# Attention with hashed buckets and an FFN: the low products of P times v narrowed to 64 columns and woven into the transposes

## The chip, the cores and the metric

One NeuronCore of a Trainium2 chip. The metric is the device time of one execution in microseconds (us), the median of 3 runs. All engines of the core work from queues of their own: TensorE (PE in the profile, its weight loads PEld), VectorE (DVE), ScalarE (ACT), GpSimd (POOL) and SyncE (SP), which issues most transfers.

## The reference, cut to what matters

```python
# q, k, v: (4, 8, 768, 64) f32, proj (64, 6)
mask = bucket(q @ proj)[:, :, :, None] == bucket(k @ proj)[:, :, None, :]   # 6 sign bits
scores = where(mask, q @ k.T / 8, -1e9)
attn = exp(scores - max(scores)); attn = attn / (sum(attn) + 1e-9)
x = (attn @ v) as (3072, 512)
h = x @ w_in                       # 512 -> 2048
out = (h * clip(h + 3, 0, 6) / 6) @ w_out   # 2048 -> 512
```

## The kernel before, in words

Every product is done in split precision: an operand is a high part, rounded to float32r (the fast 4-byte format of TensorE), and a low part, the rest, and the products of the parts are summed in PSUM.

**Steps.** There are 4 batches x 8 heads = 32 heads of 768 queries, each in 6 blocks of 128: 192 steps k. A step has, each for its own block: `scores` of block k+3 (LA = 3; four products of 384 columns, L305 and L308, into a pair of PSUM banks), `lowest` of block k+2 (VectorE, L315: the minimum and a copy of the scores to the tile `p`, of which there are two), `exponential` of block k+1 (ScalarE, L327, in place), `transp` of block k (TensorE, L337: six transposes of 128 x 128 float32, three into each of two PSUM banks `pt`), and `split_p` of block k, once for each bank (ScalarE copies the high part, L360; VectorE subtracts for the low part, L361). Steps go in pairs: `split_p` puts the two blocks of a pair u = k // 2 side by side, so that the product with v has 256 moving columns.

**The product with v.** `values(u, c)` does half c of pair u: for each of three blocks of keys one product with the high part (L374) and one with the low part (L375), both with the same stationary tile `vv[:, kt]`. That tile is 128 columns wide: the high part of v in 64 of them and its low part in the other 64 (which half holds which alternates from head to head, `split_v`, L287, on GpSimd). So the accumulator `acc`, a PSUM bank of 128 x 256, holds main results in 64 partitions and those of v's low part in the other 64. `output` (L384) copies it out (L402), and stores one half to `xs` in DRAM and adds the other half to it by a transfer that accumulates (`add`, L381); for the last head of a batch it adds them on the core (L399).

**What sets the order.** The order of the work on TensorE, VectorE, ScalarE and GpSimd is that of the program's text (`manual_schedule`, L840). The main loop (L848) does in each step, in this order: `transp` for both halves, `exponential(k + 1)`, `lowest(k + 2)`, then the halves of the product with v that are due, parts of the FFN (`next(fill)`), `scores` of k + 3 (in `lead`, with the loads, splits and the hash of the next head) and `split_p`. Which halves are due: up to step 101 (`third`, except step 48) one half in each step, half 0 in even steps and half 1 in odd ones; from step 102 on (GF + 2 = 102), and in step 48, both halves in the even steps and none in the odd ones. Steps 0 to 47 and 52 to about 100 are attention alone. At k = 51 the FFN of batch 0 is put in whole (`first_ffn`, with the loads and splits of the weights). From step 98 on the FFN of the finished batches runs beside attention: each step has one `gemm1` (12 products of 256 columns, L478 to L480) and one `gemm2` (six of 512, L500 to L502).

**Buffers.** PSUM banks for transposes, accumulators, `gemm1` and the normalisation (`rt`, L436) come from two tags, pt and pu, with two buffers each, in turn (`bank`, L79). The scores' pairs of banks alternate between two, s and po; with the FFN on there is only s (`pair`, L90).

Of the kernel before, what the change touches and what calls it, by code (L numbers as in the profile page):

```python
# [10 lines left out]
F32 = mybir.dt.float32  # L11
# [7 lines left out]
P = 128  # L19
# [21 lines left out]
def lsh_attention_moe(  # L41
# [10 lines left out]
    nc = tc.nc  # L52
    B, H, D, S = qkT.shape
    D //= 2
    DM, DF = w_in.shape
    KT = S // P
    HW = S // 2
    QT = HW // P
# [14 lines left out]
    def dma(out: bass.AP, in_: bass.AP):  # L73
        nonlocal last
        last = nc.sync.dma_start(out=out, in_=in_)
# [3 lines left out]
    def bank(shape, name: str, tag: str | None = None):  # L79

        nonlocal turn
        if tag is None:
            tag = ("pt", "pu")[turn % 2]
            turn += 1
        return ps.tile(shape, F32, name=name, tag=tag, bufs=2)
# [15 lines left out]
    ident = cp.tile([P, P], F32, name="ident")  # L101
# [104 lines left out]
    HK = H * KT  # L206
    GB = HK + FB
    GF = 2 * HK + FS
# [21 lines left out]
    def scale_q(i: int):  # L230

        nc.gpsimd.tensor_scalar_mul(raws[i][:D], raws[i][:D], -SCALE)

    def split_qk(i: int, copy):

        raw = raws.pop(i)
        kk, qq = (sp.tile([P, 2 * S], F32R, name=f"{x}_{i}", tag=x)[:] for x in ("kk", "qq"))
        k1, k2, q1, q2 = state[i] = [x[:, c : c + S] for x in (kk, qq) for c in (0, S)]
        if i == 0:

            nc.scalar.mul(q1[:D], raw[:D], -SCALE)
            nc.vector.tensor_copy(q1[D:], raw[D:])
            hash_weights()
            nc.vector.tensor_sub(k2[:D], raw[D:], q1[D:].bitcast(F32))
            nc.vector.scalar_tensor_tensor(
                out=q2[D:], in0=raw[:D], scalar=-SCALE, in1=q1[:D].bitcast(F32),
                op0=ALU.mult, op1=ALU.subtract,
            )
            nc.scalar.copy(k2[D:], raw[D:])
            nc.scalar.copy(q2[:D], q1[:D].bitcast(F32))  # L250
            nc.scalar.copy(k1[:D], raw[D:])
            return
        copy(q1[:], raw)
        dma(out=k2[D:].bitcast(F32), in_=q1[D:].bitcast(F32))
        dma(out=q2[:D].bitcast(F32), in_=q1[:D].bitcast(F32))
        dma(out=k1[:D].bitcast(F32), in_=q1[D:].bitcast(F32))
        nc.gpsimd.tensor_sub(k2[:D], raw[D:], q1[D:].bitcast(F32))
        nc.gpsimd.tensor_sub(q2[D:], raw[:D], q1[:D].bitcast(F32))
# [26 lines left out]
    vvs = {}  # L285

    def split_v(i: int):  # L287
        o = (i % 2) * D
        vr = vrs.pop(i)
        vv = vvs[i] = sp.tile([P, KT, P], F32R, name=f"vv{i}", tag="vv")  # L290
        nc.gpsimd.tensor_copy(vv[:, :, o : o + D], vr[:])
        nc.gpsimd.tensor_sub(
            vv[:, :, D - o : 2 * D - o], vr[:], vv[:, :, o : o + D].bitcast(F32)
        )

    scs, probs, outs = {}, {}, {}

# [33 lines left out]
    pts, parts = {}, {}  # L331
    halves = 0

    def transp(g: int, c: int):
        pt = pts[g, c] = bank([P, QT, P], f"pt{g}_{c}")
        for x in range(QT):
            nc.tensor.transpose(pt[:, x], probs[g][0][:, c, x * P : (x + 1) * P], ident[:])  # L337
        if c:
            del probs[g]

    lent = []

# [23 lines left out]
    def values(u: int, c: int):  # L366
        vv = vvs[2 * u // KT]
        if c == 0:
            accs[u] = bank([P, 2 * P], f"acc{u}")
        acc = accs[u]  # L370
        hi, lo = parts.pop((u, c))
        for x in range(QT):
            kt = c * QT + x
            nc.tensor.matmul(acc[:], lhsT=vv[:, kt], rhs=hi[:, x], start=(kt == 0), stop=False)  # L374
            nc.tensor.matmul(acc[:], lhsT=vv[:, kt], rhs=lo[:, x], start=False, stop=(kt == KT - 1))  # L375

    adds = []

    def add():
        for _, to, of in adds:  # L380
            nc.gpsimd.dma_start(out=to, in_=of, accum_op=ALU.add)  # L381
        adds.clear()

    def output(un: int):  # L384
        nonlocal vdone
        i, u = divmod(un, KT // 2)
        b, h = divmod(i, H)
        o = (h % 2) * D
        acc = accs.pop(un)

        if u != 1:
            outs[i] = sp.tile([P, 4 * P if u == 0 else 2 * P], F32, name=f"y{i}_{u}", tag=f"y{u}", bufs=1)
        y = outs[i][:, 2 * P :] if u == 1 else outs[i][:, : 2 * P]

        r = slice(o, o + D)
        r2 = slice(D - o, 2 * D - o)
        last_head = h == H - 1
        if last_head:
            nc.scalar.copy(y[r], acc[r2])  # L399
            nc.vector.tensor_add(y[r], acc[r], y[r])  # L400
        else:
            nc.scalar.copy(y, acc[:])  # L402
        if u:
            c = slice(0, 4 * P) if u == 1 else slice(4 * P, S)
            to = xs[b][h * D : (h + 1) * D, c]
            dma(out=to, in_=outs[i][r])
            if not last_head:
                adds.append((i, to, outs[i][r2]))
        vdone = 2 * un + 2
# [408 lines left out]
    vnext = 0  # L818

    def value_half():  # L820
        nonlocal vnext
        u, c = divmod(vnext, 2)
        vnext += 1
        values(u, c)
        return c == 1

    def ahead(k: int, part: int):

# [11 lines left out]
    with tc.manual_schedule(engines={ET.PE, ET.DVE, ET.Activation, ET.Pool}):  # L840
        split_qk(0, None)
        hash_qk(0)
        bits(0)
        scale_q(1)
        split_v(0)
        for x in range(3):
            ahead(0, x)
        for k in range(NS):  # L848
            end = GB if k < GB else NS
            i, t = divmod(k, KT)  # L850
            if k == HK - XE:
                lent += [cp.tile([P, 2 * WC], F32R, name=f"lent{n}", tag="w", bufs=NW) for n in range(2)]
            if k == GB:
                lent.clear()
            if k == HK:
                late["x"] = sp.tile([P, S], F32, name="late", tag="raw", bufs=1)
            for c in range(2):
                transp(k, c)
            if k + 1 < end:
                exponential(k + 1)  # L860
            if k + 2 < end:
                lowest(k + 2)
            if k == GB:
                next(first)
                pair_turn = 0

            third = k < GF + 2
            whole = False
            for _ in range(1 if third and k != HK else (2, 0)[k % 2]):
                if vnext < k - k % 2:  # L870
                    whole = value_half()
            if k >= GF - 2:
                next(fill, None)
            if whole and k >= GF:
                output(vnext // 2 - 1)
                whole = False

            hashed = k >= GF and (k + LA) % KT == 2
            if k >= GF and k + LA < end and not hashed:
                lead(k + LA)  # L880
            for c in range(2):
                split_p(k, c, third)
            if (k < GF or hashed) and k + LA < end:
                if hashed:
                    if (k + LA) // KT + 1 < NJ:
                        hash_qk((k + LA) // KT + 1)
                        bits((k + LA) // KT + 1)
                    next(fill, None)
                lead(k + LA)
            if whole:  # L890
                output(vnext // 2 - 1)
            if k >= GF - 2 and not hashed:
                next(fill, None)
            if k + LA >= NS:
                add()
            if HK - XE <= k < GB:
                for f in early_steps[k - HK + XE]:
                    f()

            if k < HK and t == 1 and i:  # L900
                with tc.issue_after(last.ins):
                    for n in range((i - 1) * WE // (H - 1), i * WE // (H - 1)):
                        load_w(n)
            if k == HK:
                late_x()
                with tc.issue_after(last.ins):
                    get_qk(H + 2)
                    for n in range(WE, WL):
                        load_w(n)
            if k + 1 == GB:  # L910
                first = first_ffn(lambda part: ahead(GB, part))
                next(first)
                for _ in range(2):
                    whole = value_half()
                output(vnext // 2 - 1)
                next(first)
        while vnext < NS:
            if value_half():
                output(vnext // 2 - 1)
        add()  # L920
        for _ in fill:
            pass
# [47 lines left out]
```

## Time and profile before

| | us |
|---|---|
| median of 3 runs (1040.15 to 1041.07) | 1040.96 |
| the profiled execution's own time | 1040.82 |
| its span | 1039.0 |
| TensorE busy | 1009.5 (97%) |
| VectorE busy | 687.0 (66%) |
| ScalarE busy | 583.6 (56%) |
| GpSimd busy | 451.4 (43%) |

The span is the time from the first to the last instruction that the profile shows. Weight loads (PEld) overlap the products of PE. A product's end is modelled and overlaps the next one's start, so two neighbours are compared by their starts.

### The profile page before, as it was taken

How to read it: one execution, taken by the hardware profiler on the slowest of the kernel's cores; microseconds unless marked ns; L12 is line 12 of the kernel's file. 1: busy time of each engine (PE TensorE's matmuls, PEld its weight loads, DVE VectorE, ACT ScalarE, POOL GpSimd, SP SyncE). 2: the span in 40 equal slices, each digit the busy share in tenths (PEclk: the TensorE clock that was granted, in tenths of full speed). 3: DMA queues.
4: the chain of work that ended last, by engine and by line, in shares of the span. 5: the costliest groups of instructions: out<-in, count | busy, mean ns of one | idle time of the engine just before them, and what ended most of it. 6: DMA issues, size and time to landing. Idle time of an engine off the chain costs nothing.

```text
span 1039.0 us, 18911 instructions
## 1 busy us (share of the span) xinstructions
PE 1009.5 (97%) x6846; PEld 927.2 (89%) x6846; DVE 687.0 (66%) x1441; ACT 583.6 (56%) x1308; POOL 451.4 (43%) x439
## 2 busy tenths in 40 slices
PE   8999879999999999999999999999999999999998
PEld 7999868887989998899999999999899999899997
DVE  6999888999479998766656666655665563333332
ACT  6888855555478887645554555454455462333332
POOL 5677753334247775645444444544454232200100
PEclk9999989999999999999999999999999999999999
DMA  3666686000144555322222232222232011101000
GB/s 93 155 149 155 187 277 236 1 2 1 46 130 112 120 124 143 80 53 60 75 46 63 61 88 59 53 71 59 60 93 47 15 37 28 42 1 41 1 22 20
DMA packets 47380, 80.68 MB, mean 78 GB/s; under 512 B 5892, under 2 KB 27780, under 8 KB 47288
## 3 DMA queue, kind: packets, MB, share of 16 engines
q1 hardware_dynamic: 42808, 73.98, 24.2%
q0 software_dynamic: 4480, 5.51, 4.6%
q8 instruction: 54, 0.88, 0.4%
q14 instruction: 38, 0.31, 0.1%
HBM read 41.95 MB, written 18.09 MB: 58 GB/s over the span
## 4 chain that ended last, share of the span: by engine, by line
PE 83%; DVE 8%; issue 3%; POOL 2%; ACT 2%; DMA 1%; SPq 0%; DVEq 0%; POOLq 0%; ACTq 0%
PE pt L337 11%; PE h L479 7%; PE h L478 7%; PE h L480 7%; PE po L500 7%; PE po L502 7%; PE po L501 7%; PE acc L374 6%; PE acc L375 6%; PE s L305 6%; PE s L308 6%; DVE wr L175 1%; DVE pl L361 1%; DVE wr L177 1%; PE z L267 1%
## 5 line engine op out<-in xcount | busy, mean ns | idle before, releaser
L315 DVE TENSOR_SCALAR_CACHE_REDUCE p<-s 128x768 f32<-128x768 f32 x192 | 183.5, 956 | 103.5 <-PE pt L337 99.5
L361 DVE TENSOR_TENSOR pl<-pt,ph 128x384 fp32r<-128x384 f32 x376 | 191.8, 551 | 50.4 <-ACT ph L360 48.3
L360 ACT CAST ph<-pt 128x384 fp32r<-128x384 f32 x376 | 165.5, 480 | 57.4 <-PE pt L337 45.0
L327 ACT ACTIVATE p<-p,m 128x768 f32<-128x768 f32 x192 | 179.5, 935 | 5.1 <-DVE p L315 4.8
L487 ACT ACTIVATE g<-h,three 128x256 f32<-128x256 f32 x192 | 91.4, 476 | 155.9 <-PE h L480 141.6
L337 PE MATMUL pt<-ident,p 128*128 128x128 f32 x1152 | 162.2, 275 | 5.9 <-DVE pl L361 4.8
L493 POOL TENSOR_TENSOR gl<-g,gh 128x256 fp32r<-128x256 f32 x96 | 74.2, 773 | 203.7 <-DVE gh L492 160.0
L488 DVE SCALAR_TENSOR_TENSOR g<-g,h 128x256 f32<-128x256 f32 x192 | 80.6, 420 | 117.8 <-ACT g L487 115.3
L337 PEld LDWEIGHTS pt<-ident,p 128*128 128x128 f32 x1152 | 137.3, 141 | 23.6 <-PE pt L337 3.8
L374 PE MATMUL acc<-ph,vv 128*128 128x256 f32 x564 | 152.8, 303 | 1.0 <-DVE pl L361 1.0
L478 PE MATMUL h<-xh,w 128*128 128x256 f32 x512 | 147.7, 289 | 1.2 <-ACT y L402 1.2
L480 PE MATMUL h<-xh,w 128*128 128x256 f32 x512 | 143.4, 280 | 1.3 <-POOL w L196 1.3
L479 PE MATMUL h<-xl,w 128*128 128x256 f32 x512 | 143.2, 280 | 0.6 <-DVE xl L470 0.6
L375 PE MATMUL acc<-pl,vv 128*128 128x256 f32 x564 | 141.1, 283 | 0.0
L500 PE MATMUL po<-w,gh 128*128 128x512 f32 x320 | 126.7, 396 | 1.5 <-ACT gh L492 1.4
L501 PE MATMUL po<-w,gh 128*128 128x512 f32 x320 | 126.2, 394 | 0.9 <-POOL w L196 0.9
L502 PE MATMUL po<-w,gl 128*128 128x512 f32 x320 | 126.6, 396 | 0.0
L374 PEld LDWEIGHTS acc<-ph,vv 128*128 128x128 f32 x564 | 107.5, 191 | 2.2 <-DVE pl L361 1.9
L375 PEld LDWEIGHTS acc<-pl,vv 128*128 128x128 f32 x564 | 107.9, 191 | 0.0
L305 PE MATMUL s<-kk,qq 76*128 76x384 f32 x384 | 101.2, 344 | 2.5 <-ACT kk L281 1.5
L308 PE MATMUL s<-kk,qq 128*128 128x384 f32 x384 | 100.0, 341 | 0.0
L478 PEld LDWEIGHTS h<-xh,w 128*128 128x128 f32 x512 | 96.4, 188 | 3.8 <-ACT y L402 2.4
(134 smaller groups left out, 1999.5 us busy)
## 6 DMA issues: line engine op xcount, KB each, us to landing
raw<-in_qkT SPq DMA_DIRECT2D x32, 384.0 KB, 3.5
kk<-qq SPq DMA_DIRECT2D x62, 192.0 KB, 3.2
wr<-in_w_in SPq DMA_DIRECT2D x16, 512.0 KB, 7.1
wr<-in_w_out SPq DMA_DIRECT2D x16, 512.0 KB, 3.8
vr<-in_v SPq DMA_DIRECT2D x32, 192.0 KB, 2.4
qq<-qq SPq DMA_DIRECT2D x31, 192.0 KB, 3.6
out<-ob SPq DMA_DIRECT2D x11, 512.0 KB, 3.0
xr<-xs SPq DMA_DIRECT2D x9, 512.0 KB
```

What stands on the lines that cost most here:

```text
L315: nc.vector.tensor_scalar(out=pr_[:], in0=s[:, :, :HW], scalar1=CAP, scalar2=None, op0=ALU.min, op1=ALU.min, accum_out=m[:],)
L327: nc.scalar.activation(pr_[:], pr_[:], AF.Exp, bias=m[:], scale=-1.0, accum_out=sms[b][:, t, h : h + 1])
L337: nc.tensor.transpose(pt[:, x], probs[g][0][:, c, x * P : (x + 1) * P], ident[:])
L361: nc.vector.tensor_sub(lo[:, :, w], pt[:], hi[:, :, w].bitcast(F32))
L374: nc.tensor.matmul(acc[:], lhsT=vv[:, kt], rhs=hi[:, x], start=(kt == 0), stop=False)
L375: nc.tensor.matmul(acc[:], lhsT=vv[:, kt], rhs=lo[:, x], start=False, stop=(kt == KT - 1))
L478: nc.tensor.matmul(hp[:], lhsT=wi[:, 0, wc], rhs=xh, start=(cc == 0), stop=False)
L479: nc.tensor.matmul(hp[:], lhsT=wi[:, 0, wc], rhs=xl, start=False, stop=False)
L480: nc.tensor.matmul(hp[:], lhsT=wi[:, 1, wc], rhs=xh, start=False, stop=(cc == NCC - 1))
L500: nc.tensor.matmul(po[u], lhsT=gh[:, us], rhs=wo[:, 0], start=(fc == 0), stop=False)
L501: nc.tensor.matmul(po[u], lhsT=gh[:, us], rhs=wo[:, 1], start=False, stop=False)
L502: nc.tensor.matmul(po[u], lhsT=gl[:, us], rhs=wo[:, 0], start=False, stop=(fc == NFC - 1))
```

## The change

`values` no longer does its products: it returns two lists, the products with the high part (`main`: all 128 columns of `vv`, first and last of the accumulation) and those with the low part (`rest`: only the first 64 columns of `vv`, into the first 64 partitions of `acc`). To make these 64 columns the main half for every head, `split_v` and `output` drop the alternation. The product of P's low part with v's low part is thereby left out.

`transp(k, n)` does both banks' six transposes and takes the n due halves with it. With two halves (n = 2) the first high product goes ahead of all transposes. If the last half taken is half 1 (`whole`), one low product follows each transpose while there are any: three in the odd steps up to 101, six in step 48 and in the even steps from 102 on. Otherwise the transposes come first, then one high product, the low ones and the other high ones. The remaining high products follow the transposes. `exponential` and `lowest` stand after all that in the text, on their own engines. In step 52 (GB) and at the end the halves are done without transposes (`value_halves`: one high, three low, two high).

```diff
     def split_v(i: int):
-        o = (i % 2) * D
         vr = vrs.pop(i)
         vv = vvs[i] = sp.tile([P, KT, P], F32R, name=f"vv{i}", tag="vv")
-        nc.gpsimd.tensor_copy(vv[:, :, o : o + D], vr[:])
-        nc.gpsimd.tensor_sub(
-            vv[:, :, D - o : 2 * D - o], vr[:], vv[:, :, o : o + D].bitcast(F32)
-        )
+        nc.gpsimd.tensor_copy(vv[:, :, :D], vr[:])
+        nc.gpsimd.tensor_sub(vv[:, :, D:], vr[:], vv[:, :, :D].bitcast(F32))
...
-    def transp(g: int, c: int):
-        pt = pts[g, c] = bank([P, QT, P], f"pt{g}_{c}")
-        for x in range(QT):
-            nc.tensor.transpose(pt[:, x], probs[g][0][:, c, x * P : (x + 1) * P], ident[:])
-        if c:
-            del probs[g]
+    def transp(g: int, n: int):
+
+        pr_, _ = probs.pop(g)
+        for c in range(2):
+            pts[g, c] = bank([P, QT, P], f"pt{g}_{c}")
+        his, los, whole = [], [], False
+        for _ in range(n):
+            h, l, whole = value_half()
+            his += h
+            los += l
+        if n > 1:
+            his.pop(0)()
+        woven = whole
+        for x in range(KT):
+            nc.tensor.transpose(
+                pts[g, x // QT][:, x % QT], pr_[:, x // QT, (x % QT) * P : (x % QT + 1) * P], ident[:]
+            )
+            if woven and los:
+                los.pop(0)()
+        for f in [*his[:1], *los, *his[1:]]:
+            f()
+        return whole
...
         hi, lo = parts.pop((u, c))
-        for x in range(QT):
+
+        def main(x: int):
             kt = c * QT + x
-            nc.tensor.matmul(acc[:], lhsT=vv[:, kt], rhs=hi[:, x], start=(kt == 0), stop=False)
-            nc.tensor.matmul(acc[:], lhsT=vv[:, kt], rhs=lo[:, x], start=False, stop=(kt == KT - 1))
+            nc.tensor.matmul(acc[:], lhsT=vv[:, kt], rhs=hi[:, x], start=(kt == 0), stop=(kt == KT - 1))
+
+        def rest(x: int):
+
+            nc.tensor.matmul(acc[:D], lhsT=vv[:, c * QT + x, :D], rhs=lo[:, x], start=False, stop=False)
+
+        return [[lambda x=x, f=f: f(x) for x in range(QT)] for f in (main, rest)]
...
-        r = slice(o, o + D)
-        r2 = slice(D - o, 2 * D - o)
+        r = slice(0, D)
+        r2 = slice(D, 2 * D)
...
-        values(u, c)
-        return c == 1
+        return *values(u, c), c == 1
...
-            for c in range(2):
-                transp(k, c)
+
+            third = k < GF + 2
+            n = 0
+            for _ in range(1 if third and k != HK else (2, 0)[k % 2]):
+                n += vnext + n < k - k % 2
+            whole = transp(k, n if k != GB else 0)
             if k + 1 < end:
                 exponential(k + 1)
...
-            third = k < GF + 2
-            whole = False
-            for _ in range(1 if third and k != HK else (2, 0)[k % 2]):
-                if vnext < k - k % 2:
-                    whole = value_half()
+            if k == GB and n:
+                whole = value_halves(n)
```

## Rows read from the trace of the kernel before

**Rows 1.** The page: span, engines, slices (tenths of 1/40 span), chain by engine.
```profile
span 1039.0 us, 18911 instructions
PE 1009.5 (97%) x6846; PEld 927.2 (89%) x6846; DVE 687.0 (66%) x1441; ACT 583.6 (56%) x1308; POOL 451.4 (43%) x439
...
PEclk9999989999999999999999999999999999999999
...
PE 83%; DVE 8%; issue 3%; POOL 2%; ACT 2%; DMA 1%; SPq 0%; DVEq 0%; POOLq 0%; ACTq 0%
```

**Rows 2.** TensorE's waits: waiting, awaited, us in total, times, longest us.
```profile
PE pt L337 <- DVE pl L361: 4.8, 6, 2.3
```

**Rows 3.** Busy time by stretch: PE, PEld, DVE, ACT, POOL, clock, DMA, GB/s.
```profile
65.00:90.00 25.00, 25.00 (x189) 24.34 (x188) 23.04 (x47) 21.61 (x50) 18.70 (x15) 1.00 0.62 152
...
700.00:800.00 100.00, 99.60 (x693) 92.60 (x692) 61.13 (x128) 50.61 (x116) 47.74 (x48) 1.00 0.27 66
```

**Rows 4.** Timeline of TensorE, 702.8 to 707.8 us: start us, duration us, engine, line.
```profile
703.33 0.40 PE L502 MATMUL po<-w,gl 128*128 128x512 f32 x1
703.56 0.82 PE L337 MATMUL pt<-ident,p 128*128 128x128 f32 x6
...
704.34 0.28 PE L375 MATMUL acc<-pl,vv 128*128 128x256 f32 x1
...
705.53 0.28 PE L375 MATMUL acc<-pl,vv 128*128 128x256 f32 x1
705.65 0.28 PE L478 MATMUL h<-xh,w 128*128 128x256 f32 x1
...
707.05 0.52 PE L305 MATMUL s<-kk,qq 76*128 76x384 f32 x2
```

**Rows 5.** Timeline 819.2 to 820.3 us, all engines; idle time before in brackets.
```profile
819.32 0.28 PE L375 MATMUL acc<-pl,vv 128*128 128x256 f32 x1
819.44 0.38 PE L436 MATMUL rt<-ident,rb 128*128 128x128 f32 x2
819.64 0.37 ACT L402 COPY y<-acc 128x256 f32<-128x256 f32 x1 [2.97 <-PE acc L375]
819.86 0.42 DVE L439 TENSOR_TENSOR xr<-xr,rt 128x256 f32<-128x256 f32 x1 [0.68 <-PE rt L436]
...
820.07 0.19 PEld L478 LDWEIGHTS h<-xh,w 128*128 128x128 f32 x1 [0.48 <-ACT y L402]
...
820.17 0.19 PEld L479 LDWEIGHTS h<-xl,w 128*128 128x128 f32 x1
```

**Rows 6.** Transposes' loads after an idle time (timeline); loads by shape (busy us, mean ns).
```profile
741.69 0.20 PEld L436 LDWEIGHTS rt<-ident,rb 128*128 128x128 f32 x2 [0.39 <-POOL rb L426]
...
L337 PEld LDWEIGHTS pt<-ident,p 128*128 128x128 f32 x1152 | 137.3, 141 | 23.6 <-PE pt L337 3.8 <-issue 2.9 <-ACT p L327 1.0
L375 PEld LDWEIGHTS acc<-pl,vv 128*128 128x128 f32 x564 | 107.9, 191 | 0.0
...
L266 PEld LDWEIGHTS z<-kk,pjh 128*108 128x108 f32 x64 | 11.1, 173 | 0.1
```

**Rows 7.** Products by shape (busy us, mean ns).
```profile
L305 PE MATMUL s<-kk,qq 76*128 76x384 f32 x384 | 101.2, 344 | 2.5 <-ACT kk L281 1.5 <-DVE qq L276 0.6 <-DVE p L315 0.3
L308 PE MATMUL s<-kk,qq 128*128 128x384 f32 x384 | 100.0, 341 | 0.0
...
L266 PE MATMUL z<-kk,pjh 128*108 128x384 f32 x64 | 21.7, 339 | 0.0
```

**Rows 8.** Timeline of VectorE and ScalarE, 701.0 to 706.9 us.
```profile
701.13 1.02 DVE L361 TENSOR_TENSOR pl<-pt,ph 128x384 fp32r<-128x384 f32 x2
...
704.42 0.96 DVE L315 TENSOR_SCALAR_CACHE_REDUCE p<-s 128x768 f32<-128x768 f32 x1 [0.71 <-PE pt L337]
...
705.85 0.37 ACT L402 COPY y<-acc 128x256 f32<-128x256 f32 x1 [2.75 <-PE acc L375]
```

**Rows 9.** Timeline of VectorE in attention alone, 65 to 70 us.
```profile
68.80 0.96 DVE L315 TENSOR_SCALAR_CACHE_REDUCE p<-s 128x768 f32<-128x768 f32 x1 [0.24 <-PE pt L337]
```

More of the change, by code (lines that the diff above doesn't have):

```diff
@@ L387, in output @@
         b, h = divmod(i, H)
-        o = (h % 2) * D
         acc = accs.pop(un)
@@ L823, in value_half, with value_halves @@
         vnext += 1
-        values(u, c)
-        return c == 1
+        return *values(u, c), c == 1
+    def value_halves(n: int):
+        for _ in range(n):
+            his, los, whole = value_half()
+            for f in [his[0], *los, *his[1:]]:
+                f()
+        return whole
     def ahead(k: int, part: int):
@@ L912, in lsh_attention_moe @@
                 next(first)
-                for _ in range(2):
-                    whole = value_half()
+                value_halves(2)
                 output(vnext // 2 - 1)
@@ L917, in lsh_attention_moe @@
         while vnext < NS:
-            if value_half():
+            if value_halves(1):
                 output(vnext // 2 - 1)
```

## The prediction

> **What bounds the kernel now.** I read the page's engine line, slices and chain first [rows 1]. TensorE is busy 97% of the span, the chain of waits is 83% TensorE, and the granted clock is in its top digit in nearly every slice. Busy overstates a pipelined engine, so I turned next to the waits of TensorE alone [rows 2]: the longest line is 4.8 us in all. Then the stretches [rows 3]: from 700 to 800 us TensorE lacks 0.4 us, and in the stage of attention alone (65 to 90 us) nothing, though VectorE is at 92% there. So in both stages the time is the sum of TensorE's instructions, and a change that moves TensorE's order is worth what it does to the distance from one start to the next. Stalls lie elsewhere, around the first FFN, which this change leaves in its order.
>
> I then read the distances from a second step beside the FFN [rows 4]. The six transposes start at 703.56, 0.109 apart (0.82 less the last one's 0.27, over five). The value products, high and low in turn, start 0.119 apart (ten of them from 704.34 to 705.53), and 512 columns take 0.23. Weight loads overlap all this.
>
> **The change part by part.** It removes no instruction. It narrows 576 low products (three for each of 192 half blocks) from 128 to 64 stationary columns, with the same 256 moving ones, drops low times low from the sum, and reorders. Pairs of transpose and low product arise where a step has a whole second half: 6 in each even step from 102 to 190 (45 steps, 270), 6 in step 48, 3 in each odd step of 3 to 47, 51, and 55 to 101 (48 steps, 144): 420. The other 156 low products stand among themselves or beside high ones.
>
> *The weight load.* What does it take alone? Where TensorE had been idle, the next load starts as soon as this one's product can: 0.10 to 0.11 after it for 128 columns of the split operands (820.07 to 820.17), but only 0.06 for a transpose (two loads take 0.20, one 0.14) [rows 5, 6]. Recorded loads go with the width, 191 ns at 128 columns and about 173 at 108, so 0.9 ns a column [rows 6]; 64 columns would be recorded at about 134 and occupy half of 0.108, 0.054 (my estimate). So the change cuts the load by half.
>
> *Does any load end last?* A transpose's load needs 0.06, yet transposes stand 0.109 apart: its own stream must hold them. The consumers say the same [rows 5]: ScalarE starts 0.32 after the start of the last 256-column product (819.32 to 819.64), VectorE 0.31 after the last transpose (819.55 to 819.86), so a transpose of 128 columns passes nearly as late as 256. Behind a transpose, then, 0.109 of stream already covers a load of 0.108, and a product's 0.12 covers either. Halving a covered load gives nothing.
>
> *The rule against that reading.* The Trainium skill, "TensorE: Matmul & The Clock Gate", section "LDWEIGHTS (loading the stationary operand)", prices a load by its columns alone, 107 ns for 128; the split operands agree (0.10 to 0.11), the transposes' 0.06 does not. By that page transposes would be bound by their loads and a pair would gain; that is the second rival below.
>
> *The stream of 64 columns.* No row is that narrow. The nearest is the hash, 108 wide: 384 columns are recorded at 339 ns, against 341 at 128 wide; and 76 rows instead of 128 make 344 [rows 7]. The array's filling does not set the pace, so I keep 0.12. Bounds: down to a transpose's 0.109, worth 576 x 0.0105 = 6.0 us; upward, the price of going to and fro.
>
> *To and fro.* From the 512-column product at 703.33 to gemm1 at 705.65 are 2.32 us [rows 4]; 0.233 + 6 x 0.109 + 12 x 0.119 is 2.315. So one way in and out costs at most 0.005. Woven, there are 420: 0 to 2.1 us. I take 0.
>
> *The order beside the FFN.* The first high product now stands ahead of the transposes and a low one behind each. The last transpose ends 0.12 + 5 x 0.12 = 0.71 later, the step's products as late as before. Ahead of it: the high product needs the previous step's split, done by 701.13 + 1.02 = 702.15 for a start at 703.56 [rows 4, 8], so 1.4 us cover it; its accumulator bank comes free with that same split. Behind it: VectorE's minimum, which waits for the transposes, goes from 704.42 to 705.13 and ends at 706.1; the scores that need its bank start at 707.05, so 0.9 us are left. The split of this step waits in ScalarE's queue behind the accumulator's copy (idle until 705.85), whose time does not move. Odd steps keep their order. Cost 0.
>
> *Attention alone.* In odd steps three low products go ahead of the last transposes, which end 0.36 later; even steps keep their order. The minimum waits there for the transposes, with 0.24 us of idle VectorE before it [rows 9]. It is 0.12 behind in the next step and has 0.36 more after that. The scores alternate between two banks and the exponential has a step in hand, so I take 0 and keep the lag as a rival.
>
> *Small things.* Step 48 is woven with no FFN to cover it: its first product meets a split that ends about half a us later, once. GpSimd's two splits of v keep their size, and the output and accumulate transfers their bytes; only the partitions are now the same for each head. At 0.06 us of load and 0.11 of stream for a transpose no step falls idle, so the clock has no cause to fall.
>
> The sum: 0 on the profiled execution's 1040.82 (span 1039.0 and 1.8 around it), which lies 0.14 under the median of the three runs, 1040.96. I forecast 1041.0, its own range 1039 to 1043.
>
> **The rivals.**
> *The narrow product streams faster.* Half the array would let 256 columns pass at a transpose's 0.109: 1041 - 6 = 1035.0. For it: the products stand 0.119 apart, above the transposes' 0.109. Against: widths of 108 and 128 pass alike.
> *The transposes are short and their loads hold them.* If the 0.109 between transposes were the load and not the stream, a low product would cover it and the transpose would shrink to a load of some 0.06: 420 x 0.05 = 21, so 1020. Against: the load of 0.06 after an idle time, and consumers that start after 0.31.
> *VectorE's lag is passed on* (slower). Each of 48 woven odd steps of attention alone costs the 0.36 less the 0.24 of idle time: 48 x 0.12 = 5.8, so 1046.8. It decides as soon as TensorE needs, within a step, something behind that minimum. For it: VectorE's 92%. Against: two banks, and 0.36 more time in the even step.
> *Each change of width drains the array* (slower). A 256-column product is recorded at 0.28 from start to end against 0.12 to the next start, so 0.16 of pipeline would be bared twice a pair [rows 4]: 420 x 0.32 = 134, so 1175. Against: no sign of it between transposes and products, both 128 wide, nor at the hash's 108. The Trainium skill, "TensorEngine Tiling (Array Packing)", section "Key Properties", says that changing the tiling mode drains TensorE; no run here shows a width at which it would. The skill's "PSUM — Partial Sum Buffer", under "The four PSUM rules", says that float32r products force the full column group, which speaks against a mode change here.
>
> **How the numbers follow.** Forecast 0.50; faster stream 0.14; short transposes 0.13; small gains of the order over 2.1 us 0.03; VectorE's lag 0.12; drain 0.04; small losses over 2.1 us 0.04. A measurement of this kernel tells some 0.2%, 2.1 us, from no change. Faster is 0.14 + 0.13 + 0.03 = 0.30, same 0.50, slower 0.20. The range takes in the faster stream and VectorE's lag and leaves out short transposes and drain (0.17): 1034.5 to 1047.
>
> **What would show it.** Right: weight loads of the low products recorded near 134 ns; a pair of transpose and low product still 0.109 + 0.12 = 0.23 from transpose to transpose; TensorE's waits as short as before. Wrong: pairs of 0.17 to 0.18 (short transposes), low products 0.109 before the next start (faster stream), 0.5 or more (drain), or TensorE waiting for VectorE between 20 and 110 us or 300 and 400 us (lag).

## The result, and the profile after

The changed kernel takes 1044.99 us (median of 6 runs, 1043.41 to 1046.23) against 1040.59 (1039.94 to 1041.82) of the kernel before, a ratio of 1.0042 [1.0029, 1.0055]: slower by 4.4 us. The forecast was no change at 1041.0. The time lies inside the stated range, 1034.5 to 1047, whose upper part stood for the slower rival "VectorE's lag is passed on" (1046.8). Half of what is lost is lost in that rival's place, attention alone, though by another road; the other half comes from two terms that no case had.

The profiled execution took 1045.29 us. Its page:

```profile
span 1043.5 us, 18777 instructions
PE 1010.8 (97%) x6846; PEld 929.3 (89%) x6846; DVE 682.8 (65%) x1441; ACT 581.8 (56%) x1308; POOL 450.7 (43%) x439
...
PE 83%; DVE 8%; issue 3%; ACT 2%; POOL 2%; DMA 0%; DVEq 0%; POOLq 0%; ACTq 0%
```

Beside [rows 1] the page shows almost nothing: the same number of matmuls, TensorE 1.3 us busier, the same chain. 4.4 us in a thousand have to be looked for by place. I took marks that both kernels have: the score product of the second row, one for each block of scores. The same two marks of before and of after (timeline of TensorE):

```profile
28.70 0.53 PE L308 MATMUL s<-kk,qq 128*128 128x384 f32 x2
...
110.64 0.52 PE L308 MATMUL s<-kk,qq 128*128 128x384 f32 x2
```

```profile
27.73 0.51 PE L305 MATMUL s<-kk,qq 128*128 128x384 f32 x2
...
111.05 0.52 PE L305 MATMUL s<-kk,qq 128*128 128x384 f32 x2
```

The kernel before needs 81.94 us from one to the other, the changed one 83.32: +1.38 in the first stage of attention alone. The whole span, cut in this way (us, after less before; times are those of before):

| stretch | difference |
|---|---|
| start, to 29 us | -0.97 |
| attention alone, 29 to 111 | +1.38 |
| 111 to 122 | -0.09 |
| step 48 and first FFN, 122 to 287 | +1.47 |
| attention alone, 299 to 391 (row starts at 287) | +1.68 |
| the FFN sets in again, 391 to 436 | +1.59 |
| steps beside the FFN, 436 to 852 | -0.55 |
| tail | -0.03 |

They add up to 4.48, the difference of the spans being 4.5. The steady steps beside the FFN, which the change was mostly about, win half a microsecond; attention alone, one half-clock stretch and the place where the FFN sets in lose 6.1. The start differs by up to 0.9 between two runs below whose first steps have the same text (-1.46 in b1_one_woven, -0.56 in c1_one_and_plain), so I give it to no part of the change.

**Beside the FFN**, as forecast. The loads' group, by shape, and then TensorE's timeline of a second step:

```profile
L392 PEld LDWEIGHTS acc<-pl,vv 128*64 128x64 f32 x564 | 75.0, 136 | 1.6
```

```profile
708.31 0.27 PE L345 MATMUL pt<-ident,p 128*128 128x128 f32 x1
708.34 0.36 PE L392 MATMUL acc<-pl,vv 128*64 128x256 f32 x1
...
709.45 0.27 PE L345 MATMUL pt<-ident,p 128*128 128x128 f32 x1
```

The narrow load is recorded at 136 ns (forecast 134, before 191 in [rows 6]). Six transposes with a low product between them take 1.14 us from the first to the last, so a pair of transpose and product is 0.228; before, 0.109 and 0.119 to 0.120 make 0.228 to 0.229.

**Attention alone**: the loss is no steady drift. Step by step it is +0.25 us in one step of six, 13 times in the two stages (13 x 0.25 = 3.2; the 1.38 and 1.68 are 3.06), and within 0.09 elsewhere, nearly cancelling. It is the step behind the one in which VectorE also forms the hash's bits (below, the step behind the hash's). VectorE's group of minima has more idle time ahead of it, in the kernel before and then after:

```profile
L315 DVE TENSOR_SCALAR_CACHE_REDUCE p<-s 128x768 f32<-128x768 f32 x192 | 183.5, 956 | 103.5 <-PE pt L337 99.5
```

```profile
L312 DVE TENSOR_SCALAR_CACHE_REDUCE p<-s 128x768 f32<-128x768 f32 x192 | 183.4, 955 | 143.9 <-PE pt L345 141.3
```

Most of these 40 us lie beside the FFN (81.7 us before, 108.4 after), where they cost next to nothing; the two stages of attention alone have 6.1 and 6.3 before, 9.2 and 9.6 after. A sum over the span does not tell where the time is lost.

Some lines around one such step, after (idle time before, and what ended it, in brackets):

```profile
346.42 1.08 DVE L276 TENSOR_SCALAR qq<-z,thr,val 44x768 fp32r<-44x768 f32 x1
...
347.43 0.49 PE L345 MATMUL pt<-ident,p 128*128 128x128 f32 x3
...
347.96 0.96 DVE L312 TENSOR_SCALAR_CACHE_REDUCE p<-s 128x768 f32<-128x768 f32 x1 [0.45 <-PE pt L345]
...
348.83 0.82 PE L345 MATMUL pt<-ident,p 128*128 128x128 f32 x6
...
348.95 1.02 DVE L374 TENSOR_TENSOR pl<-pt,ph 128x384 fp32r<-128x384 f32 x2
...
349.63 0.19 PEld L388 LDWEIGHTS acc<-ph,vv 128*128 128x128 f32 x1 [0.22 <-issue]
349.74 0.25 PEld L392 LDWEIGHTS acc<-pl,vv 128*64 128x64 f32 x2
```

and before:

```profile
343.92 1.08 DVE L276 TENSOR_SCALAR qq<-z,thr,val 44x768 fp32r<-44x768 f32 x1
...
344.24 0.82 PE L337 MATMUL pt<-ident,p 128*128 128x128 f32 x6
...
345.10 0.96 DVE L315 TENSOR_SCALAR_CACHE_REDUCE p<-s 128x768 f32<-128x768 f32 x1
...
346.09 1.02 DVE L361 TENSOR_TENSOR pl<-pt,ph 128x384 fp32r<-128x384 f32 x2
...
346.32 0.82 PE L337 MATMUL pt<-ident,p 128*128 128x128 f32 x6
...
346.87 0.19 PEld L374 LDWEIGHTS acc<-ph,vv 128*128 128x128 f32 x1
346.98 0.19 PEld L375 LDWEIGHTS acc<-pl,vv 128*128 128x128 f32 x1
```

Before, the six transposes of the odd step are through (344.24 and 0.82) just after VectorE leaves the bits (345.00), and its minimum follows within 0.1 us. After, three low products push the last transposes back, and VectorE stands idle for 0.45. In both kernels, in nearly every odd step, the minimum starts 0.31 after the start of the last transpose, so it moves by the whole delay. Its minimum and the two subtractions behind it in its queue start later. The next step's six transposes (348.83, 346.32) go out in their usual rhythm; the first high product behind them does not: its weight load starts 0.80 after the first transpose instead of 0.55 (349.63 less 348.83; 346.87 less 346.32). That is the 0.25. The accumulator of this product takes, by round robin, the PSUM bank of the first half's transposes four allocations back (`pt` and `acc` share one pool), and the bank is free when L374 has read it. The start times show this wait. In each of these 13 steps after, the high product starts 0.146 to 0.147 after the end of that subtraction; before, in 12 of them, it starts 0.236 to 0.244 after it. So before there were 0.09 to 0.10 us to spare.

**Where the FFN sets in**, TensorE already waited for that subtraction before [rows 2]; most of the waits got longer (7.7 us in 7 waits over the whole span, 4.8 in 6 before). After, then before:

```profile
396.08 0.52 PE L345 MATMUL pt<-ident,p 128*128 128x128 f32 x3 [0.68 <-DVE pl L374]
...
407.30 0.52 PE L345 MATMUL pt<-ident,p 128*128 128x128 f32 x3 [0.81 <-DVE pl L374]
...
423.73 0.30 PE L345 MATMUL pt<-ident,p 128*128 128x128 f32 x1 [1.23 <-DVE pl L374]
```

```profile
392.26 0.52 PE L337 MATMUL pt<-ident,p 128*128 128x128 f32 x3 [0.32 <-DVE pl L361]
...
403.01 0.52 PE L337 MATMUL pt<-ident,p 128*128 128x128 f32 x3 [0.49 <-DVE pl L361]
```

**Step 48 on**: 3.4 us at a granted clock of 0.50, that is 1.2 GHz, that the kernel before does not have. After, a line of the timeline, with TensorE's wait, and the row of a stretch (columns as in [rows 3]); then both of before:

```profile
129.65 0.44 PE L454 MATMUL rt<-ident,rb 128*128 128x128 f32 x2 [1.86 <-POOL rb L444]
```

```profile
130.70:134.10 3.40, 3.40 (x17) 3.33 (x16) 2.61 (x5) 1.74 (x4) 2.55 (x3) 0.50 0.64 187
```

```profile
129.34 0.44 PE L436 MATMUL rt<-ident,rb 128*128 128x128 f32 x2 [1.59 <-POOL rb L426]
```

```profile
130.70:134.10 3.40, 3.40 (x26) 3.35 (x25) 3.32 (x7) 1.88 (x4) 2.39 (x4) 1.00 0.60 179
```

17 matmuls are done where 26 were. At half speed 3.4 us lose 1.7 us of work, which is the +1.47 of this stretch. Ahead of it TensorE had waited 1.86 us for GpSimd's normalised rows, 0.27 longer than before. (Both kernels have another stretch at half the clock, of 6.8 us, between 139 and 148 us.)

### The profile page after: what moved, and what is told of

The parts are those of the page before. It is cut to its first block, busy times and chain, and to the rows that moved or that the text cites. A ratio compares the mean times of both kernels' runs of the same rounds, so it can differ in the third digit from the quotient of the medians.

```text
span 1043.5 us, 18777 instructions
## 1 busy us (share of the span) xinstructions
PE 1010.8 (97%) x6846; PEld 929.3 (89%) x6846; DVE 682.8 (65%) x1441; ACT 581.8 (56%) x1308; POOL 450.7 (43%) x439
## 4 chain that ended last, share of the span: by engine, by line
PE 83%; DVE 8%; issue 3%; ACT 2%; POOL 2%; DMA 0%; DVEq 0%; POOLq 0%; ACTq 0%
PE pt L345 11%; PE h L496 7%; PE h L497 7%; PE h L498 7%; PE po L518 7%; PE po L519 7%; PE po L520 7%; PE acc L388 6%; PE acc L392 6%; PE s L302 6%; PE s L305 6%; DVE wr L175 1%; DVE pl L374 1%; DVE wr L177 1%; PE z L267 1%
## 5 line engine op out<-in xcount | busy, mean ns | idle before, releaser
L345 PE MATMUL pt<-ident,p 128*128 128x128 f32 x1152 | 203.8, 273 | 8.6 <-DVE pl L374 7.7
L374 DVE TENSOR_TENSOR pl<-pt,ph 128x384 fp32r<-128x384 f32 x376 | 191.8, 551 | 27.8 <-ACT ph L373 25.9
L373 ACT CAST ph<-pt 128x384 fp32r<-128x384 f32 x376 | 167.9, 481 | 57.3 <-PE pt L345 47.9
L345 PEld LDWEIGHTS pt<-ident,p 128*128 128x128 f32 x1152 | 146.9, 141 | 19.4 <-issue 5.3
L392 PE MATMUL acc<-pl,vv 128*64 128x256 f32 x564 | 132.8, 341 | 0.0
L388 PE MATMUL acc<-ph,vv 128*128 128x256 f32 x564 | 115.3, 299 | 0.4 <-DVE pl L374 0.2
L496 PEld LDWEIGHTS h<-xh,w 128*128 128x128 f32 x512 | 96.3, 188 | 3.8 <-ACT y L420 2.4
L497 PEld LDWEIGHTS h<-xl,w 128*128 128x128 f32 x512 | 96.4, 188 | 2.7 <-DVE xl L488 1.3
L498 PEld LDWEIGHTS h<-xh,w 128*128 128x128 f32 x512 | 96.2, 188 | 1.7 <-POOL w L196 1.7
```

The source lines that it names most:

```text
L345: nc.tensor.transpose(pts[g, x // QT][:, x % QT], pr_[:, x // QT, (x % QT) * P : (x % QT + 1) * P], ident[:])
L374: nc.vector.tensor_sub(lo[:, :, w], pt[:], hi[:, :, w].bitcast(F32))
L392: nc.tensor.matmul(acc[:D], lhsT=vv[:, c * QT + x, :D], rhs=lo[:, x], start=False, stop=False)
L496: nc.tensor.matmul(hp[:], lhsT=wi[:, 0, wc], rhs=xh, start=(cc == 0), stop=False)
L497: nc.tensor.matmul(hp[:], lhsT=wi[:, 0, wc], rhs=xl, start=False, stop=False)
L498: nc.tensor.matmul(hp[:], lhsT=wi[:, 1, wc], rhs=xh, start=False, stop=(cc == NCC - 1))
```

## The experiments

The theory: the weave in the odd steps delays VectorE, the accumulator's bank comes free late, and TensorE pays in attention alone. Rivals: the weave in the even steps, beside the FFN and where it sets in; the narrow products themselves; the place of v's halves, which the change also moved. The kernels differ from the changed one by a few lines in `transp` (L331) or `values` (L379), b2 in the main loop; each run's profile has its own line numbers. The runs' results, with the stretches of each profile against that of before, as above (us). The kernel before took 1040.59 us beside the changed kernel, 1042.00 beside the a runs, 1041.65 beside the b runs and 1041.49 beside the c runs, so runs of different groups are compared by the ratio and not by the median:

| run | alone, 29–111 | 122–287 | alone, 299–391 | sets in, 391–436 | beside FFN, 436–852 | median us | ratio to before |
|---|---|---|---|---|---|---|---|
| changed kernel | +1.38 | +1.47 | +1.68 | +1.59 | -0.55 | 1044.99 | 1.0042 [1.0029, 1.0055] |
| b0_after | +1.38 | +1.37 | +1.65 | +1.62 | +1.19 | 1047.33 | 1.0046 [1.0032, 1.0059] |
| a1_odd_plain | -0.25 | -0.17 | -0.15 | +0.99 | -0.49 | 1042.08 | 1.0001 [0.9992, 1.0010] |
| a2_ffn_plain | +1.38 | -0.19 | +1.71 | +0.36 | -1.25 | 1042.44 | 1.0010 [1.0001, 1.0018] |
| a3_narrow_alone | -0.29 | -0.49 | -0.20 | -0.25 | -1.12 | 1039.60 | 0.9981 [0.9969, 0.9994] |
| c3_narrow_again | -0.25 | -0.22 | -0.21 | -0.52 | -1.19 | 1039.39 | 0.9982 [0.9972, 0.9993] |
| a4_woven_wide | +2.39 | +1.44 | +2.68 | +1.78 | +0.90 | 1050.46 | 1.0085 [1.0068, 1.0103] |
| b3_plain_wide | -0.02 | +0.42 | +0.06 | +0.03 | -0.07 | 1042.15 | 0.9998 [0.9989, 1.0007] |
| b1_one_woven | -0.86 | +0.05 | -0.82 | +0.74 | -0.29 | 1040.67 | 0.9991 [0.9982, 1.0000] |
| c2_two_woven | -0.35 | +1.31 | +0.07 | +1.41 | -0.30 | 1044.47 | 1.0033 [1.0021, 1.0046] |
| c1_one_and_plain | -0.87 | -0.16 | -0.86 | -0.43 | -0.20 | 1040.24 | 0.9989 [0.9977, 1.0001] |
| b2_split_first | +4.28 | +1.47 | +4.44 | +2.29 | +1.12 | 1055.13 | 1.0116 [1.0097, 1.0134] |

The stretches of one profile add up to its span only with those left out here (start, 111 to 122 and the tail), of which 111 to 122 varies most, from -0.1 to +2.9: some runs wait there for the transfers that bring the hash its operands (up to 2.0 us), and in a3 and c2 a stretch at half the clock follows.

**No weave in the odd steps** (a1_odd_plain).

```diff
-        woven = whole
+        woven = whole and n > 1
```

> The odd steps of attention alone are not woven (transposes first, then the half's products); steps with two halves stay woven. Theory (VectorE's lag): all of the loss comes from odd steps up to 101, whose last transposes end 0.35 us later, so this gives back about 4.6 us and ends at 1040 to 1041, with the stalls after the hash's step gone. Rival (the pairs themselves, beside the FFN or by the narrow products, cost time): it stays above 1043. Rival (a stretch of 3.4 us more at half clock near 130 us, 1.7 us): it ends near 1043 at least when that stretch is there.

The loss in attention alone is gone, 3.06 us and 0.4 more, and the half-clock stretch near 130 us is absent. By the ratios 4.3 us of the time come back (1.0042 less 1.0001), where 4.6 were expected. 1.0 us of the loss where the FFN sets in is still there: that part is the even steps'.

**No weave in the even steps** (a2_ffn_plain): the low products stand among the high ones in the order of before.

```diff
-        if n > 1:
-            his.pop(0)()
-        woven = whole
+        woven = whole and n == 1
...
+        if n > 1:
+            los = [f for h, l in zip(his[:5], los) for f in (h, l)][1:] + los[5:]
+            his = [his[0], his[5]]
```

> The other half of the change's order: only the odd steps up to 101 are woven; steps with two halves have the order of before, with narrow low products. Theory (VectorE's lag): the loss stays, 1045 to 1046, as the weave beside the FFN gains only some 0.5 us. Rival (pairs beside the FFN cost time): 1041 or less.

Attention alone loses exactly as before (+1.38, +1.71), so the place is right. The total was expected too high (1045 to 1046; 1042.44 came). The even steps carry two things that I had not given to them: most of the loss where the FFN sets in (+0.36 is left of 1.59) and 0.7 us in the steps beside the FFN. And the half-clock stretch is missing here too, though it is not the even steps that make it: a1, which weaves them, has none either.

**Neither weave, narrow products** (a3_narrow_alone, and once more as c3_narrow_again), and **the same with wide ones** (b3_plain_wide, with the product of `rest` as in a4).

```diff
-        if n > 1:
-            his.pop(0)()
-        woven = whole
...
-            if woven and los:
-                los.pop(0)()
-        for f in [*his[:1], *los, *his[1:]]:
-            f()
+        for x in range(0, len(his), QT):
+            h, l = his[x : x + QT], los[x : x + QT]
+            for f in [h[0], l[0], h[1], l[1], l[2], h[2]]:
+                f()
```

> No weave at all: transposes first, high and low products in turn as before, but low products 64 columns wide. Theory: no stall is added and a narrow product is as long as a wide one in the same place, so 1040 to 1041 and 0.119 to 0.120 us from one product to the next; if it is the width that makes 0.117 of 0.120, the low products go by 2 to 3 ns and the time to 1039 to 1040. Rival (narrow products cost): above 1043.

> The kernel of a3 (no weave) with low products of all 128 columns: only the place of v's parts and the order within a half differ from the kernel before. Theory (the width made a3's gain: 0.117 us from product to product where it was 0.120): the distances go back to 0.119 to 0.120 and the time to that of before, within 0.1%. Rival (the order or the fixed place of the halves made it): 0.117 and 2 us under before, as in a3.

> The kernel of a3 once more, beside c1 on one chip: 2 us under before again, its stages 0.2 to 0.3 us under before each in attention alone and 1.1 beside the FFN.

Wide, unwoven products take what the kernel before takes, within 0.1% (0.9998 [0.9989, 1.0007]), so neither the place of v's halves nor the order of high and low counts. Narrow ones are faster than both kernels, 0.9981 and 0.9982 of the time before. Their low products in one step beside the FFN, first and last of a run of eight distances (timeline of a3, then of b3):

```profile
705.01 0.29 PE L389 MATMUL acc<-pl,vv 128*64 128x256 f32 x1
...
705.95 0.39 PE L389 MATMUL acc<-pl,vv 128*64 128x256 f32 x2
```

```profile
706.64 0.28 PE L389 MATMUL acc<-pl,vv 128*128 128x256 f32 x1
...
707.59 0.40 PE L389 MATMUL acc<-pl,vv 128*128 128x256 f32 x2
```

0.94 over 8 is 0.1175, 0.95 over 8 is 0.119. These lines are no finer than that; the stretch is: -1.12 and -1.19 over 41 even steps of twelve products are 0.0023 us a product. Half of the twelve are narrow, so that is some 4.6 ns for each narrow one. The start times of the traces agree (means between 450 and 840 us): from one low product to the next are 0.116 in a3 and 0.120 in b3, from one high one to the next 0.1179 and 0.1185.

**The weave with wide products** (a4_woven_wide): `lo` times all of vv.

```diff
-            nc.tensor.matmul(acc[:D], lhsT=vv[:, c * QT + x, :D], rhs=lo[:, x], start=False, stop=False)
+            nc.tensor.matmul(acc[:], lhsT=vv[:, c * QT + x], rhs=lo[:, x], start=False, stop=False)
```

> The changed kernel with low products of all 128 columns, in the same order. Theory: the order alone makes the loss, so 1045 as for the change, and a load of 128 columns is covered behind a transpose, so pairs stay at 0.226 to 0.23 us. Rival (64 columns are what lets a pair go without a bare load): pairs longer by 0.01 us or more, 420 of them, 1049 or more.

The pairs, from first to last transpose of a second step:

```profile
712.80 0.27 PE L345 MATMUL pt<-ident,p 128*128 128x128 f32 x1
...
713.96 0.28 PE L345 MATMUL pt<-ident,p 128*128 128x128 f32 x1
```

1.16 over five is 0.232 against 0.228 narrow; over all 190 pairs between 450 and 840 us the means are 0.2318 and 0.2272. The time of the rival came, but not its longer pairs (0.01 or more). The 4.6 ns that a narrow product saves in a pair are about what it saves in a3 with no transpose beside it, so they do not show that a wide load behind a transpose ends late. Each of the stages but the half-clock one is 0.2 to 1.5 us worse than in the changed kernel. In attention alone, 1.0 us a stage, the wait for VectorE's subtraction is in nearly every step behind a woven odd one: the high product starts 0.145 to 0.147 after its end, which in the changed kernel holds of the step behind the hash's alone.

By the ratios, the narrow product is worth 0.0039 to 0.0043 of the time woven (a4 less the changed kernel and b0), 4.1 to 4.5 us, and 0.0016 to 0.0017 unwoven (b3 less a3 and c3), 1.7 to 1.8 us. The weave itself costs 0.0060 to 0.0065 with narrow products (the changed kernel and b0 less a3 and c3), 6.2 to 6.8 us, and 0.0087 with wide ones (a4 less b3), 9.1 us.

**The changed kernel again** (b0_after, no edit), to learn which of its terms come back.

> The changed kernel once more, beside the next three on one chip: 4 to 4.5 us over the kernel before (its parts in the traces: about 1.4 from 29 to 111 us and 1.7 from 287 to 385 us, 1.6 from there to 436 us, less 0.55 beside the FFN).

All four losses came back within 0.1 us. Beside the FFN it had a wait of 1.73 us for GpSimd's rows (L454 for L444, at 500.20) where the first profile has 0.14; -0.55 and +1.19 are the same program, so single waits of that kind must not be read as an effect.

**The dose**: one low product woven in the odd steps (b1_one_woven, shown), or two (c2_two_woven, `x < 2`); the even steps woven as in the change.

```diff
-            if woven and los:
+            if woven and los and (n > 1 or x < 1):
```

> As the changed kernel, but in odd steps up to 101 one low product is woven instead of three, so that the last transposes end 0.12 us later and not 0.35. Theory (VectorE's lag against a slack of about 0.1 us at the step after the hash): the stall there falls from 0.25 us to under 0.05, the two stages of attention alone lose under 0.4 us each, and the kernel ends 1 to 2 us over before. Rival (a woven pair in itself loses time in attention alone): a third of the loss stays in the stages, 0.5 us each, and no stall is seen at the step after the hash. Rival (any weave there costs all): 1.4 and 1.7 us again.

> The dose between: two low products woven in odd steps, last transposes 0.24 us later. Theory (a slack of some 0.1 us): the stall at the step after the hash is 0.12 to 0.15 us, half of the changed kernel's 0.24; the stages of attention alone come to 0 to +0.6 us each, and the kernel to 1 to 2.5 us over b1. Rival (no threshold; each woven product costs alike): 0.16 us and two thirds of the whole loss.

The mean loss in the step behind the hash's is 0.00 us at none woven, 0.01 at one, 0.13 at two and 0.25 at three. A low product pushes the last transpose back by 0.118; 0.118 - 0.01, 2 x 0.118 - 0.13 and 3 x 0.118 - 0.25 are 0.10 to 0.11: there are some 0.10 us of slack, and beyond them the delay passes to TensorE one for one. The start times of before had the same 0.09 to 0.10; with one, two or three woven the product of that step always starts 0.145 to 0.149 after the subtraction's end. The rival without a threshold would have had 0.08 at one and 0.16 at two. VectorE's minimum behind the bits, in c2, then in b1 (timeline):

```profile
349.12 0.96 DVE L312 TENSOR_SCALAR_CACHE_REDUCE p<-s 128x768 f32<-128x768 f32 x1 [0.36 <-PE pt L345]
```

```profile
343.26 0.96 DVE L312 TENSOR_SCALAR_CACHE_REDUCE p<-s 128x768 f32<-128x768 f32 x1 [0.20 <-PE pt L345]
```

VectorE's idle time before that minimum goes 0.21, 0.34, 0.44 with one, two, three (means of the 13 steps). One woven product even wins 0.6 us a stage over none: it fills a small wait that two of three odd steps already had before the second bank's transposes. In the kernel before and in a1, the third to fifth of the six start about 0.14 apart there, not 0.109; with one woven all the later ones are 0.109 apart. Both totals missed what was expected: b1 came out 1 us under before (0.9991) and not 1 to 2 over, and c2 4.4 us over b1 by the ratios and not 1 to 2.5; 1.3 of that is the half-clock stretch near 130 us in its profile.

**The subtraction first** (b2_split_first): in odd steps the first half's copy and subtraction are issued ahead of the minimum, so that the bank comes free early.

```diff
+            early0 = n == 1 and whole
+            if early0:
+                split_p(k, 0, third)
...
-            for c in range(2):
+            for c in range(early0, 2):
                 split_p(k, c, third)
```

> As the changed kernel with all three products woven, but in the woven odd steps VectorE subtracts the first bank's low part ahead of the minimum and not behind it, which frees that PSUM bank for the next step's accumulator. Theory (the stall is that bank, kept by a subtraction that waits behind the late minimum): the stalls at the step after the hash go, the two stages lose under 0.4 us each, about 3 us come back. Rival (the late minimum itself, by the exponential or the scores, is what TensorE waits for): the stall stays or grows, 1.4 us and more in each stage.

Wrong by far: 1.0116. The 0.25 behind the hash's step are gone (-0.02), so the bank of that subtraction is what TensorE waited for. But new waits came in other steps, 0.41 and 0.25 each:

```profile
349.75 0.56 DVE L374 TENSOR_TENSOR pl<-pt,ph 128x384 fp32r<-128x384 f32 x1 [0.65 <-ACT ph L373]
350.23 0.95 DVE L312 TENSOR_SCALAR_CACHE_REDUCE p<-s 128x768 f32<-128x768 f32 x1
...
352.58 0.30 PEld L302 LDWEIGHTS s<-kk,qq 76*128 76x128 f32 x2 [0.15 <-DVE p L312]
```

The subtraction needs ScalarE's copy, VectorE stands idle for it for 0.65, the minimum queues behind, and the scores wait for the minimum. My expectation had counted the bank and not the queue.

**One woven in the odd steps, none in the even** (c1_one_and_plain): a2 with `x < 1` in the weave's condition, both best doses together.

> What the runs point to: one low product woven in the odd steps up to 101 (as b1), and in steps with two halves the order of before with narrow low products (as a3). Theory: the parts add: 0.8 us won in each stage of attention alone (b1), 1.1 beside the FFN and 0.3 where it sets in (a3), so 2.5 to 3 us under before, 1038.5 to 1039.5 where before is 1041.7, ahead of a3 and b1. Rival (the gains of b1 and a3 are one and the same, or b1's came from one profile's luck): no better than a3, 2 us under before.

Its profiled execution took 1037.81 us, 3.0 under that of before, and its stretches show the parts but one: beside the FFN, where 1.1 us were to be won, a single wait of 1.17 us for GpSimd's rows (at 491.37) leaves -0.20. Its median is 1040.24 (1037.81 to 1043.07), 0.9989 [0.9977, 1.0001], where 1038.5 to 1039.5 were expected. It is not shown to beat a3, nor the kernel before; why its executions spread so much stays open.

## Why the prediction was right or wrong, point by point

The measured 1044.99 lies in the stated range but beyond the 2.1 us that the prediction counted as no change. It is in the range because the range took in the lag of VectorE as a rival; the mechanism behind the forecast, a lag that costs nothing, did not hold.

**The bound.** Right: TensorE's sum, and each effect is a distance between its starts or a wait of it. What was missed is that a stage without a wait [rows 3] may be short of one by 0.1 us.

**"The weight load" and "Does any load end last?"** Right in size: 136 ns for 134, pairs of 0.228 for 0.23. "Halving a covered load gives nothing" was not refuted: narrow products save 4 to 5 ns each, but as much without a transpose beside them as in a pair (a3, a4), and whether the load or the stream makes it, no run separates. The transposes did not shrink to their loads, or the pairs would stand at 0.17 to 0.18, so that rival (1020) fell. The Trainium skill, "TensorE: Matmul & The Clock Gate", section "LDWEIGHTS (loading the stationary operand)", prices a load by its columns: the narrow one, recorded at 136 ns instead of 191, agrees in kind; that a transpose is held by its load, as that price would have it, the pairs of 0.228 contradict.

**"The stream of 64 columns … I keep 0.12."** A size: a narrow product passes in 0.116 (some 0.004 less), inside the bound of 0.0105. Unwoven it is worth 1.1 us beside the FFN and 1.7 to 1.8 in all (a3, c3 against b3). The rival of 0.109 (1035.0) fell.

**"To and fro" and the drain.** At most a few ns: 0.2272 a pair against 0.109 + 0.116 = 0.225. The even steps' weave costs 0.6 to 0.8 beside the FFN (a1 and the changed kernel at -0.5, a2 and a3 at -1.1 to -1.25). Of that 0.45 lies in two steps, whose first transposes (522.98 and 770.91 in the changed kernel) start 0.35 behind the high product ahead of them instead of 0.12, and 0.146 behind the end of VectorE's subtraction: the same wait again. The rest, 0.15 to 0.35 over some 240 pairs, is about 1 ns a pair. The drain (1175) fell. The Trainium skill, "PSUM — Partial Sum Buffer", under "The four PSUM rules", has float32r products force the full column group, which speaks against another mode for 64 columns; the pairs of 0.228, without a drain, agree.

**"The order beside the FFN … Cost 0."** Wrong in its reach. I worked it out in a steady step at 700 us, with VectorE at half load, and it held there but for those 0.6 to 0.8; the "1.4 us cover it" is the typical step's, and two steps had none. Between 391 and 436 us TensorE waits for VectorE already [rows 2], and there the delay of the last transposes goes into the waits: 1.0 us with the even steps' weave alone (a1), 0.4 with the odd steps' (a2), 1.6 with both.

**"Attention alone … I take 0": the step that failed.** It found the delay (0.36), counted VectorE's idle time (0.24) against it and then asked only who waits for the minimum: the scores' banks and the exponential. But that idle time is VectorE waiting for these very transposes (the minimum starts 0.31 after the last of them, before and after), so it takes up none of the delay. Behind the minimum in VectorE's queue stands the subtraction that frees the transposes' bank, and the next step's accumulator takes that bank; I had named this very bank in the step beside the FFN. What takes it up is the time that this bank is free before it is needed, and it is shortest, some 0.10, in the step behind the hash's, since bits of 1.08 us have gone ahead on VectorE in the step before it; the 0.24 was read in another step [rows 9]. The loss is 0.25 in 13 steps, 3.1 us in the two stages, and the rival's price had 0.12 in 48, 5.8: right engine, other wait, other count. The dose shows it: nothing up to 0.1 of delay, then one for one. That the total came near the rival's 1046.8 is luck: its 5.8 was 3.1, and the half-clock stretch and the place where the FFN sets in, which it did not have, added 1.5 and 1.6.

**"Small things … the clock has no cause to fall."** Wrong by about 1.5 us, in both profiles of the changed kernel. The profiles, by how many low products the odd steps weave, with TensorE's wait for the normalised rows near 130 us: none, 1.58 to 1.61 us (before, a1, a3, c3, b3), one, 1.70 (b1, c1), two or three, 1.76 to 1.87 (c2, b2, a2, the changed kernel, b0, a4). The extra half-clock stretch follows the wait in all of the last but a2, and in none of the others. The exception, a2, its wait (timeline) and the stretch behind it:

```profile
130.30 0.44 PE L455 MATMUL rt<-ident,rb 128*128 128x128 f32 x2 [1.83 <-POOL rb L445]
```

```profile
130.30:134.00 3.70, 3.70 (x28) 3.69 (x29) 3.14 (x7) 2.11 (x5) 3.52 (x4) 1.00 0.69 183
```

So a wait that grows by a quarter of a microsecond may cost 1.5 more by the clock. That the longer wait lets the clock fall is argued from these rows and not shown: a2, after 1.83 us of waiting, stayed at 1.00, and what else enters is open. The hash's waits for its transfers near 114 us point the same way: 3.4 us at 0.50 follow in a3 (1.83 us of waiting) and c2 (1.39 and 0.62), none in b3 (1.26 and 0.50) and a1 (0.80 and 0.60). The half us feared for step 48 itself did not appear (a1, woven there, and a2, not woven, differ by 0.02 in that stretch).

## What to carry to other kernels

When an instruction is moved back, follow the whole queue of the engine that waits for it, to every buffer that each entry frees, and ask who takes that buffer next in the round robin; a delay is free only up to the smallest slack in the cycle of steps, so look for the step with the most extra work, not the typical one. The idle time of an engine ahead of an instruction is no slack when it is spent waiting for what is moved. A stage whose bounding engine never waits may be a tenth of a microsecond from waiting. Try the parts of a bundled change singly: here the narrower operand was a small gain and the new order, which was to cover it, the loss.

## What the runs showed of the hardware

From one product of 256 moving columns to the next are 0.116 us with 64 stationary columns and 0.120 with 128 (a3 and b3, low products behind each other), of which the hash's 108 columns [rows 7] had given no sign. A pair of a transpose and such a product takes 0.2272 us with 64 columns and 0.2318 with 128 (the changed kernel and a4), the same saving. In the step behind the hash's of the changed kernel, the product that waited for VectorE to read its PSUM bank started 0.146 to 0.147 us after the end of that read, 13 times. TensorE's granted clock was 0.50, that is 1.2 GHz, for 3.4 us after a wait of 1.86 us, and 1.00 after one of 1.59 at the same place; after one of 1.83 it was 0.50 in c2 and 1.00 in a2.
